# Step stores laid out per column group, two buffers for tile partials and an earlier ride load in a memory-augmented attention and SwiGLU training kernel

## The chip, the cores and the metric

The kernel runs on one core of a Trainium2 chip. The metric is the device time of one execution in microseconds (us). The engines of the core are named as in the profile: PE is the matrix engine (PEld its weight loads), DVE the vector engine, ACT the scalar engine, POOL the GpSimd engine and SP the engine that issues most transfers. Sixteen DMA engines move data between HBM and the on-chip memories.

## What is computed

The reference is a forward pass and its gradients. All tensors are bf16, with 2048 tokens of width 640, 32 heads of 128, segments of 32 tokens and 8 memory rows.

```
xn = layernorm(x)
mem = mem0                                  # 8 rows
for s in range(64):                         # segments of 32 tokens
    h = concat([mem, xn[32*s : 32*s+32]])   # 40 rows
    q, k, v = h @ Wq, h @ Wk, h @ Wv        # 32 heads
    p = softmax(mask(q @ k.T * scale))      # memory rows see all 40 rows,
    o = (p @ v) @ Wo                        # token rows those up to their own
    mem = o[:8]                             # the next segment's memory
    outs.append(o[8:])
g = silu((silu(xn @ w1) * (xn @ w3)) @ w2)
out = x + concat(outs) * g
# outputs: out and the gradients of x, mem0, Wq, Wk, Wv, Wo, w1, w3, w2 for grad_out
```

Each segment's memory comes out of the segment before, so the 64 steps are a chain, forward and, in the gradients, backward.

## The kernel before, in words

The kernel is a sequence of phases: layer norm, the gated part forward, attention forward (`phase3_Afwd`), its output (`phase3b_out`), attention backward (`phase4_Abwd`), the weight gradients of attention (`phase6_Awgrads`) and the gated part backward.

**Attention forward.** Tokens 0 to 671 get their q, k and v in an opening stage and are kept in `QVX` and `KX`. Then come 64 steps. In step `t` the function `chain` takes `hx`, 32 columns: the 8 memory rows of this segment, and 24 token rows that *ride* along, from token 672 on. `packed_half` multiplies them with half of a weight matrix so that the 128 partitions of a PSUM bank hold four groups of 32 rows: group g, row r at partition 32g + r, for columns of group g (1024 columns each). Two halves of 512 columns fill one staging tile `stg` of 128 x 1024 (lines 452 to 458), of which there are two buffers: `sk` for keys, `sq` for queries, and `sv` for values, which takes the buffer of `sk`. `dump` (line 455) stores a staging tile to DRAM on SP's queue: `sk` to `KS[t]` (467), `sq` and `sv` to the two halves of `QVS[t]` (477, 523).

From the staging tiles `packed_sel` turns the memory rows into `kT` and `qmT`; the first and second half of `sv` are copied by ACT (476, 481), and from there 8 copies on DVE fill the first rows of `vt` (484). Then follow the memory rows' scores (489), their copy `sTm` on ACT (491), two transposes (497), the maximum on DVE (499), exp, sum, `Pm` (509), transposes (514), the product with `vt` (520), the output projection `packed_out` (531), and `fold_add` and `fold_turn`, which give the next step's memory columns of `hx`. At the end `vt` gets the next segment's token rows (529).

Between these pieces stand calls `gap(...)`. They insert work on the 96 tokens of a tile of three segments (a *quad* is four heads of one tile): loads of k, q and v rows (`ld_k`, `ld`), transposes, scores, softmax, products. Those loads read the stored rows of three or four steps at once, 512 columns wide (`m_src`, `x_src`, which is `tok_src`). `in_order` at the end fixes the written order on each engine and on each queue.

**Attention backward** has the same form, from step 63 down to 0. Its opening stage (lines 766 to 790) loads the transposed weights (`WoT` first) and computes the token rows of the gradient from token 1344 on into `GX0`. Before the steps, `turn`, `dprob`, `dsoft` and `gmem_ld` run through the first 19 quads; the rest is put into the gaps. In `chain` the tile `sg` of 128 x 1024 is filled by DVE and ACT (879, 881), turned (883 to 887), and stored to `GOS[t]` (888). `loads(t - 1)` (917) brings the next step's `vT`, `Pm` and `Qst` (the queries of the memory rows, from `QVS`), `load_k(t - 1)` (933) its key rows, and `ride(t - 1)` (934) does two things: in every fourth step it loads 96 token columns into `gride` on SP's queue, and in every step POOL copies 24 of them to `gox`, the input of the next step. `gmem` (1016) computes a quad's share in the memory rows' gradients, copies it on ACT to `gks` (1025 to 1028, one buffer) and stores it to `GXP` (1029); after it, `ld_next` loads the quad four places on (`gqv`, `gor`, `gPr`, line 959). In a step, this happens in the gaps W1, G4 and G5.

Of the kernel before, what the change touches and what calls it, by code (L numbers as in the profile page):

```python
# [9 lines left out]
BF16 = mybir.dt.bfloat16  # L10
F32 = mybir.dt.float32
# [5 lines left out]
P = 128  # L17
# [23 lines left out]
class K:  # L41
# [110 lines left out]
    def setup_dram(self):  # L152
        tc = self.tc
        S, D, T, H, F = self.S, self.D, self.T, self.H, self.F
        HD = self.HD
# [14 lines left out]

        self.QVS = mk("QVS", (T, 32, 2, HD))
        self.KS = mk("KS", (T, 32, HD))
        self.GOS = mk("GOS", (T, 32, HD))
        self.NB0 = 672
# [7 lines left out]
        for tl in range(self.NTL):  # L182
# [3 lines left out]
            ns, nm = self.geo(tl)[0:2]  # L186
# [15 lines left out]
    def x_src(self, tl, w, c0, c1):  # L202
        return self.tok_src(96 * tl, self.geo(tl)[2], w, c0, c1)

    def tok_src(self, x0, nx, w, c0, c1):
        if w == "k":
            X0, XS = self.KX[:, c0:c1], self.KS[:, :, c0:c1]
        elif w == "qv":
            X0, XS = self.QVX[:, :, c0:c1], self.QVS[:, :, :, c0:c1]
        else:  # L210
            i = "qv".index(w)
            X0, XS = self.QVX[:, i, c0:c1], self.QVS[:, :, i, c0:c1]
        if x0 + nx <= self.NB0:
            return [(0, nx, X0[x0:x0 + nx])]
        out, a = [], 0
        while a < nx:
            t, r = divmod(x0 + a - self.NB0, 24)
            if r == 0 and nx - a >= 48:
                nt = (nx - a) // 24
                out.append((a, a + 24 * nt, XS[t:t + nt, 8:32]))  # L220
                a += 24 * nt
            else:
                m = min(24 - r, nx - a)
                out.append((a, a + m, XS[t, 8 + r:8 + r + m]))
                a += m
        return out

    def m_src(self, tl, w, c0, c1):
        ns = self.geo(tl)[0]
        XS = {"k": self.KS, "g": self.GOS}.get(w)  # L230
        if XS is None:
            XS = self.QVS if w == "qv" else self.QVS[:, :, "qv".index(w)]
        if w == "qv":
            return XS[3 * tl:3 * tl + ns, 0:8, :, c0:c1]
        return XS[3 * tl:3 * tl + ns, 0:8, c0:c1]

    def g_src(self, tl, c0, c1):
        nx = self.geo(tl)[2]
        x0 = 96 * tl
        if x0 >= self.GB0:  # L240
            return [(0, nx, self.GX0[x0 - self.GB0:x0 - self.GB0 + nx, c0:c1])]
        return [(0, 96, self.GOS[8 + 4 * tl:12 + 4 * tl, 8:32, c0:c1])]

# [120 lines left out]
def phase3_Afwd(k):  # L364
    nc, tc = k.nc, k.tc
    D, DC, S, H, HD, T = k.D, k.DC, k.S, k.H, k.HD, k.T
    with tc.tile_pool(name="aw", bufs=1) as wp:
# [34 lines left out]
        with tc.tile_pool(name="ast", bufs=1) as st, tc.tile_pool(name="achain", bufs=1) as ch, \  # L402
# [39 lines left out]
            def chain(t, gap):  # L442
# [12 lines left out]
                def dump(sg, dst, q=nc.sync):  # L455
                    q.dma_start(dst.rearrange("r (g c) -> g r c", g=4), sg[:])
                sk = stage()
# [18 lines left out]
                k.copy(sv[:, 0:512], bA[:], eng='s')  # L476
                dump(sq, k.QVS[t, :, 0])
                packed_half(k, bB, hx, Wv, 1)
# [43 lines left out]
                nc.vector.tensor_copy(oTm[:], pom[:])  # L522
                dump(sv, k.QVS[t, :, 1], nc.sync)
                if t + 1 == T:
# [237 lines left out]
def phase4_Abwd(k, out2):  # L762
    nc, tc = k.nc, k.tc
    D, DC, S, H, HD, T = k.D, k.DC, k.S, k.H, k.HD, k.T
    out2f = out2.flatten_outer_dims()
    with tc.tile_pool(name="gw", bufs=1) as wp:
        WoT = wp.tile([P, DC, HD], BF16, name="WoT")
        k.dma(WoT[:], k.WOT.rearrange("(dc p) j -> p dc j", p=P))
# [23 lines left out]
        with tc.tile_pool(name="gst", bufs=1) as st, tc.tile_pool(name="gchain", bufs=1) as ch, \  # L792
# [24 lines left out]

            def ride(t):
                if t < 8:
                    return  # L820
                b, sub = (t - 8) // 4, (t - 8) % 4
                if sub == 3:
                    rt = ch.tile([P, DC, 96], BF16, name="gride", tag="gride")
                    nc.sync.dma_start(rt[:], k.GST[:, 96 * b:96 * b + 96].rearrange("(dc p) s -> p dc s", p=P))
                    rides[b] = rt
                nc.gpsimd.tensor_copy(goxs[t % 2][:, :, 8:32], rides[b][:, :, 24 * sub:24 * sub + 24])

            def loads(t):
                tl, s = t // 3, t % 3
                ns, nm, nx, n = k.geo(tl)  # L830
                vT = ch.tile([P, H, 40], BF16, name="vTt", tag="vTt", bufs=1)
                nc.sync.dma_start(vT[:], k.VTD[tl][:, s])
                Pm = ch.tile([P, 2, 40], BF16, name="gPm", tag="gPm", bufs=2)
                nc.sync.dma_start(Pm[:], k.PM[t].rearrange("p (a c) -> p a c", a=2))
                Qst = ch.tile([P, 2, P], BF16, name="Qst", tag="Qst", bufs=2)
                for a in range(2):
                    nc.sync.dma_start(Qst[:, a, :], k.QVS[t, 0:8, 0, a * 2048:(a + 1) * 2048])
                ins[t] = vT, Pm, Qst

            def load_k(t):  # L840
                kr = ch.tile([40, HD], BF16, name="krow", tag="krow", bufs=1)
                nc.sync.dma_start(kr[0:8, :], k.KS[t, 0:8, :])
                k.load_x(kr, 8, k.tok_src(32 * t, 32, "k", 0, HD), nc.sync)
                krs[t] = kr

            def load_xp(t):
                xp = ch.tile([P, 8, 2, 32], F32, name="xp", tag="xp", bufs=1)
                nc.sync.dma_start(xp[:], k.GXP[t // 3, :, :, t % 3])
                xps[t] = xp
# [8 lines left out]
            def chain(t, gap):  # L858
# [27 lines left out]
                for a in range(2):  # L886
                    nc.vector.tensor_copy(gmT[:, a].rearrange("p q (g j) -> p j g q", g=2), pg[:, :, 2 * a:2 * a + 2, :])
                nc.sync.dma_start(k.GOS[t].rearrange("r (g c) -> g r c", g=4), sg[:])
                gap("W1")
# [19 lines left out]
                nc.vector.tensor_reduce(Dm[:], pr[:], axis=AX.X, op=ALU.add)  # L909
                u = ch.tile([P, 2, 40], F32, name="gu", tag="gu")  # L910
                nc.vector.tensor_tensor(u[:], ps2[:], bc_last(Dm[:], 40), ALU.subtract)
# [9 lines left out]
                for a in range(2):  # L921
                    nc.tensor.transpose(ps3[:, a, :], dS[:, a, :], k.ident[:])
                dST = ch.tile([40, 2, 8, 16], BF16, name="dSTm", tag="dSTm")
                nc.scalar.copy(dST[:].rearrange("p a q h -> p a (q h)"), ps3[:])
# [91 lines left out]
            def gmem(tl, qd):  # L1016
# [5 lines left out]
                for j in range(4):  # L1022
                    nc.tensor.matmul(pk[:, 0, j, :], qv[0:n, 0, j * P:(j + 1) * P], dS[0:n, j, 0:nm], start=True, stop=True)
                    nc.tensor.matmul(pk[:, 1, j, :], gor[0:n, j * P:(j + 1) * P], Pr[0:n, j, 0:nm], start=True, stop=True)
                ks = fl.tile([P, ns, 2, 4, 8], F32, name="gks", tag="gks", bufs=1)
                for i in range(2):
# [647 lines left out]
```

## Time and profile before

| | |
|---|---|
| median of 3 runs | 6858.57 us (6856.48 to 6860.1) |
| the profiled execution | 6865.93 us |
| its span | 6863.8 us |
| PE busy | 5507.1 us, 80% |
| PEld busy | 3209.3 us, 47% |
| DVE busy | 2423.3 us, 35% |
| ACT busy | 1884.3 us, 27% |
| POOL busy | 987.8 us, 14% |
| moved by DMA | 876.37 MB, 128 GB/s |
| mean granted PE clock | 0.883 |

How to read the rows that follow. A row of the timeline has the start and the duration in us, the engine (SPq is SP's queue of transfers), the line, the operation, what it writes and reads, how many were merged, and in brackets how long the engine had stood idle and what released it. A row of the waits has the engine and what it wanted to do, an arrow to what released it, the total in us, how often, and the longest. A row of a line or tile has the shortest, median and longest duration in ns, and the first and last start in us. In the DMA view the time asked for is cut into 40 equal slices: a digit is the share of the 16 DMA engines that were busy in that slice, in tenths, and below it stand the GB/s moved. The granted clock is 1.00 where PE ran at full speed and 0.50 where it ran at half.

### The profile page before, as it was taken

Reading aid. Unit: us, or ns where it says so; the run is one execution under the profiler, and the core shown is the slowest. Engines: PE = TensorE matmul, PEld = TensorE weight load, DVE = VectorE, ACT = ScalarE, POOL = GpSimd, SP = SyncE. Lnnn points to the kernel's source line nnn. Section 1 sums busy time; section 2 is a strip of 40 time slices with the busy share of each in tenths; the row PEclk is TensorE's granted clock in tenths of the full one; section 3 lists DMA queues with packets and bytes.
Section 4 is the critical chain, followed back from the end, with each engine's and each line's share of the span. In section 5 each row is a group of like instructions: output and inputs, shape, how many; then the busy total and the mean of one; then the engine's idle time right before and its main releaser. Section 6 shows DMA issues by size and latency. Waiting matters only on the chain. (4 is left out here: it accounts for less than half of the span.)

```text
span 6863.8 us, 167869 instructions
## 1 busy us (share of the span) xinstructions
PE 5507.1 (80%) x68068; PEld 3209.3 (47%) x68620; DVE 2423.3 (35%) x7541; ACT 1884.3 (27%) x5180; POOL 987.8 (14%) x1507
## 2 busy tenths in 40 slices
PE   6877888888886874887778884998899998775688
PEld 3444544444443543555555553555555555342244
DVE  5423544444443213444344431222222222021752
ACT  3332444433433212222222221222222222010301
POOL 0000333323233101232223320000000000000000
PEclk9888998888887886888888987999999999886799
DMA  6474444333334464665556655223322233555673
GB/s 191 149 263 120 122 120 111 103 104 104 104 106 134 124 197 113 158 157 145 142 146 164 165 129 95 78 78 95 78 79 77 77 86 87 112 155 179 194 174 94
DMA packets 1038695, 876.37 MB, mean 128 GB/s; under 512 B 525449, under 2 KB 941033, under 8 KB 1028705
## 3 DMA queue, kind: packets, MB, share of 16 engines
q1 hardware_dynamic: 656570, 568.18, 29.9%
q10 hardware_dynamic: 337894, 213.14, 11.5%
q0 software_dynamic: 43456, 84.28, 5.4%
q8 instruction: 540, 8.85, 0.6%
q14 instruction: 235, 1.92, 0.1%
HBM read 556.09 MB, written 309.09 MB: 126 GB/s over the span
## 5 line engine op out<-in xcount | busy, mean ns | idle before, releaser
L1207 PE MATMUL wg<-gr,hr 120*128 120x512 bf16 (+1 forms) x2640 | 578.4, 379 | 1.0 <-DVE ghacc L1196 0.5
L1190 PE MATMUL g<-w,gT 128*128 128x512 bf16 x1936 | 573.0, 384 | 0.7 <-ACT gT L92 0.7
L1191 PE MATMUL g<-w,gT 128*128 128x128 bf16 x2112 | 466.6, 221 | 10.7 <-issue 1.7
L1207 PEld LDWEIGHTS <-hr 120*128 120x128 bf16 (+1 forms) x2640 | 254.0, 98 | 321.4 <-issue 22.4
L1190 PEld LDWEIGHTS <-gT 128*128 128x128 bf16 x2112 | 209.0, 99 | 220.4 <-issue 13.6
L1196 DVE TENSOR_TENSOR ghacc<-ghacc,g 120x512 f32<-120x512 f32 (+1 forms) x154 | 105.9, 687 | 567.6 <-PE g L1190 567.6
L337 PEld LDWEIGHTS <-gkv 128*8 128x8 bf16 x8192 | 215.4, 100 | 162.7 <-DVE gkv L871 33.9
L92 ACT COPY gT<-t6g 128x480 bf16<-128x480 bf16 (+1 forms) x352 | 192.0, 545 | 333.8 <-PE t6g L1181 238.3
L318 PEld LDWEIGHTS <-hx 128*32 128x32 bf16 x7680 | 179.6, 96 | 175.6 <-issue 15.8
L337 PE MATMUL gbank<-WvT,gkv 128*8 128x320 bf16 x4096 | 238.6, 413 | 26.6 <-DVE gkv L871 26.6
L90 DVE CAST stg<-bank 128x512 bf16<-128x512 f32 x256 | 176.9, 691 | 222.4 <-PE bank L318 173.7
L1200 POOL CAST gxo<-ghacc 120x640 bf16<-120x640 f32 (+1 forms) x22 | 15.8, 720 | 1591.8 <-issue 1479.2
L604 ACT ACTIVATE xP<-xsp,xnm 120x120 bf16<-120x120 f32 (+1 forms) x704 | 240.2, 366 | 12.1 <-DMA PR<-xP 6.1
L484 DVE COPY vt<-stg 8x512 bf16<-8x512 bf16 x512 | 149.0, 291 | 265.9 <-ACT stg L92 259.7
L90 DVE CAST wgo<-wg 128x512 bf16<-128x512 f32 x72 | 47.5, 688 | 543.6 <-PE wg L1207 499.0
L1232 PE MATMUL oa<-gow,orr 120*128 120x512 bf16 x704 | 196.5, 382 | 36.7 <-DMA orr<-OR 36.7
L1181 PE MATMUL t6g<-ident,gr 120*128 120x120 bf16 (+1 forms) x2112 | 187.7, 219 | 43.9 <-ACT gT L92 41.7
L983 POOL DMA_DIRECT2D VTD<-gvT x176 | 127.9, 728 | 598.5 <-ACT gvT L982 581.1
L337 PE MATMUL bank<-Wo,oTm 128*8 128x320 bf16 x4032 | 209.2, 379 | 1.3
L1191 PEld LDWEIGHTS <-gT 128*128 128x128 bf16 x2112 | 208.6, 99 | 0.3
L615 POOL TENSOR_TENSOR xP<-xP,xrz 120x480 bf16<-120x480 bf16 (+1 forms) x176 | 170.2, 967 | 172.2 <-ACT xP L604 116.0
L1465 PE MATMUL w2acc<-gzB_all,hb_tok 128*128 128x128 bf16 (+3 forms) x437 | 122.8, 434 | 87.8 <-DMA hb_tok<-HB 82.7
(314 smaller groups left out, 11548.5 us busy)
## 6 DMA issues: line engine op xcount, KB each, us to landing
QVS<-stg SPq DMA_DIRECT2D x128, 256.0 KB
gqv<-QVS SPq DMA_DIRECT2D x112, 192.0 KB
vTt<-VTD SPq DMA_DIRECT2D x64, 320.0 KB
OR<-xv POOLq DMA_DIRECT2D x168, 120.0 KB, 5.5
VTD<-gvT POOLq DMA_DIRECT2D x168, 120.0 KB, 5.7
orr<-OR SPq DMA_DIRECT2D x8, 2520.0 KB
PR<-xP POOLq DMA_DIRECT2D x168, 112.5 KB, 7.6
gPr<-PR SPq DMA_DIRECT2D x168, 112.5 KB
```

The costliest lines, as they stand in the source:

```text
L90: return nc.vector.tensor_copy(out, in_)
L92: return nc.scalar.copy(out, in_)
L318: k.nc.tensor.matmul(bank[32 * g:32 * g + 32, :], x[:, dc, :], W[:, dc, c0:c0 + 512], start=(dc == 0), stop=(dc == k.DC - 1), tile_positio ...
L337: k.nc.tensor.matmul(pm[p0:p0 + nq, 0:320], x[:, h, :], W[:, h, 320 * b:320 * b + 320], start=(first and i == 0), stop=(last and i == 15), ...
L484: nc.vector.tensor_copy(vt[0:8, c0:c0 + 512], sv[32 * g:32 * g + 8, b * 512:(b + 1) * 512])
L604: nc.scalar.activation(Pb[0:n, j, 0:n], sp[0:n, j, :], ACT.Exp, bias=nmx[0:n, j:j + 1], scale=k.scale, accum_out=Z[0:n, j:j + 1])
L615: nc.gpsimd.tensor_tensor(Pb[0:n, :, 0:n], Pb[0:n, :, 0:n], bc_last(rz[0:n], n), ALU.mult)
L1181: nc.tensor.transpose(pt[:, j, :], gr[0:n, i, j * P:(j + 1) * P], k.ident[0:n, 0:n])
L1190: nc.tensor.matmul(g5[:], gT[:, i, j, :], W[:, j, 0:512], start=f, stop=l)
L1191: nc.tensor.matmul(g1[:], gT[:, i, j, :], W[:, j, 512:640], start=f, stop=l)
L1207: nc.tensor.matmul(accs[dc][:], hr[0:n, tl, dc * P:(dc + 1) * P], grs[tl][0:n, 2 - i, :], start=(tl == 0), stop=(tl == NTL - 1))
L1232: nc.tensor.matmul(ac[j][0][:], lh, gow[0:n, tl, 0:512], start=(tl == 0), stop=(tl == NTL - 1))
```

## The change

- `QVS`, `KS` and `GOS` get a dimension for the four column groups ahead of the rows. A staging tile's partition 32g + r is then row (g, r) of the tensor, and a store names one dimension of 128 rows of 1024 elements (2 KB) where it named 4 groups of 32 rows.
- All that reads these tensors goes through a new helper `step_src`. Loads of 512 columns read the same pieces as before at other addresses. Loads of whole rows (`vt`, `krow`) read four pieces of 1024 elements per row where they read one of 4096.
- The memory rows' queries are copied at the start of the backward phase from `QVS` to a new tensor `QM`, in four transfers on SP's queue, and `Qst` is loaded from there.
- `gks` gets two buffers. `gu` and `dSTm` give up buffers of their own and share those of `gpr` and `dPT`.
- `ride` is divided: `ride_ld`, the load, is issued at the gap W0 of the step before, ahead of that gap's work; the copy stays where it was.

```
-        self.QVS = mk("QVS", (T, 32, 2, HD))
-        self.KS = mk("KS", (T, 32, HD))
-        self.GOS = mk("GOS", (T, 32, HD))
+        self.QVS = mk("QVS", (T, 4, 32, 2, 1024))
+        self.KS = mk("KS", (T, 4, 32, 1024))
+        self.GOS = mk("GOS", (T, 4, 32, 1024))
+        self.QM = mk("QM", (T, 8, HD))
...
+    def step_src(self, w, t0, t1, r0, r1, c0, c1):
+        g = c0 // 1024
+        if w == "qv":
+            return self.QVS[t0:t1, g, r0:r1, :, c0 - 1024 * g:c1 - 1024 * g]
+        XS = {"k": self.KS, "g": self.GOS}.get(w)
+        if XS is None:
+            XS = self.QVS[:, :, :, "qv".index(w)]
+        if c1 - c0 > 1024:
+            assert t1 == t0 + 1 and (c0, c1) == (0, self.HD)
+            return XS[t0, :, r0:r1, :].rearrange("g r c -> r g c")
+        return XS[t0:t1, g, r0:r1, c0 - 1024 * g:c1 - 1024 * g]
...
     def m_src(self, tl, w, c0, c1):
...
+        return self.step_src(w, 3 * tl, 3 * tl + self.geo(tl)[0], 0, 8, c0, c1)
...
                 def dump(sg, dst, q=nc.sync):
-                    q.dma_start(dst.rearrange("r (g c) -> g r c", g=4), sg[:])
+                    q.dma_start(dst.rearrange("g r c -> (g r) c"), sg[:])
...
-                dump(sq, k.QVS[t, :, 0])
+                dump(sq, k.QVS[t, :, :, 0])
...
     with tc.tile_pool(name="gw", bufs=1) as wp:
+        for g in range(4):
+            nc.sync.dma_start(k.QM[:, :, g * 1024:(g + 1) * 1024], k.QVS[:, g, 0:8, 0, :])
         WoT = wp.tile([P, DC, HD], BF16, name="WoT")
...
-            def ride(t):
+            def ride_ld(t):
                 if t < 8:
                     return
                 b, sub = (t - 8) // 4, (t - 8) % 4
                 if sub == 3:
                     rt = ch.tile([P, DC, 96], BF16, name="gride", tag="gride")
                     nc.sync.dma_start(rt[:], k.GST[:, 96 * b:96 * b + 96].rearrange("(dc p) s -> p dc s", p=P))
                     rides[b] = rt
+
+            def ride(t):
+                if t < 8:
+                    return
+                b, sub = (t - 8) // 4, (t - 8) % 4
                 nc.gpsimd.tensor_copy(goxs[t % 2][:, :, 8:32], rides[b][:, :, 24 * sub:24 * sub + 24])
...
-                    nc.sync.dma_start(Qst[:, a, :], k.QVS[t, 0:8, 0, a * 2048:(a + 1) * 2048])
+                    nc.sync.dma_start(Qst[:, a, :], k.QM[t, :, a * 2048:(a + 1) * 2048])
...
-                nc.sync.dma_start(kr[0:8, :], k.KS[t, 0:8, :])
+                nc.sync.dma_start(kr[0:8, :], k.KS[t, :, 0:8, :].rearrange("g r c -> r g c"))
...
-                nc.sync.dma_start(k.GOS[t].rearrange("r (g c) -> g r c", g=4), sg[:])
+                nc.sync.dma_start(k.GOS[t].rearrange("g r c -> (g r) c"), sg[:])
...
-                u = ch.tile([P, 2, 40], F32, name="gu", tag="gu")
+                u = ch.tile([P, 2, 40], F32, name="gu", tag="gpr")
...
-                dST = ch.tile([40, 2, 8, 16], BF16, name="dSTm", tag="dSTm")
+                dST = ch.tile([40, 2, 8, 16], BF16, name="dSTm", tag="dPT")
...
-                ks = fl.tile([P, ns, 2, 4, 8], F32, name="gks", tag="gks", bufs=1)
+                ks = fl.tile([P, ns, 2, 4, 8], F32, name="gks", tag="gks", bufs=2)
...
                     if g == "W0":
+                        ride_ld(t - 1)
                         at(turn, t, 0)
...
+            ride_ld(T - 1)
             ride(T - 1)
```

More of the change, by code (lines that the diff above doesn't have):

```diff
@@ L203, in x_src @@
         return self.tok_src(96 * tl, self.geo(tl)[2], w, c0, c1)
-    def tok_src(self, x0, nx, w, c0, c1):
[L206 to L212, printed above, removed]
+    def step_src(self, w, t0, t1, r0, r1, c0, c1):
[9 more added lines that the diff above has]
+        return XS[t0:t1, g, r0:r1, c0 - 1024 * g:c1 - 1024 * g]
+    def tok_src(self, x0, nx, w, c0, c1):
         if x0 + nx <= self.NB0:
+            X0 = self.KX[:, c0:c1] if w == "k" else self.QVX[:, :, c0:c1] if w == "qv" else self.QVX[:, "qv".index(w), c0:c1]
             return [(0, nx, X0[x0:x0 + nx])]
@@ L217, in tok_src @@
             t, r = divmod(x0 + a - self.NB0, 24)
-            if r == 0 and nx - a >= 48:
+            if r == 0 and nx - a >= 48 and c1 - c0 <= 1024:
                 nt = (nx - a) // 24
-                out.append((a, a + 24 * nt, XS[t:t + nt, 8:32]))
+                out.append((a, a + 24 * nt, self.step_src(w, t, t + nt, 8, 32, c0, c1)))
                 a += 24 * nt
@@ L223, in tok_src @@
                 m = min(24 - r, nx - a)
-                out.append((a, a + m, XS[t, 8 + r:8 + r + m]))
+                out.append((a, a + m, self.step_src(w, t, t + 1, 8 + r, 8 + r + m, c0, c1)))
                 a += m
@@ L228, in m_src @@
     def m_src(self, tl, w, c0, c1):
[L229 to L235, printed above, removed]
+        return self.step_src(w, 3 * tl, 3 * tl + self.geo(tl)[0], 0, 8, c0, c1)
     def g_src(self, tl, c0, c1):
@@ L241, in g_src @@
             return [(0, nx, self.GX0[x0 - self.GB0:x0 - self.GB0 + nx, c0:c1])]
-        return [(0, 96, self.GOS[8 + 4 * tl:12 + 4 * tl, 8:32, c0:c1])]
+        return [(0, 96, self.step_src("g", 8 + 4 * tl, 12 + 4 * tl, 8, 32, c0, c1))]
     def load_x(self, dst, off, srcs, eng):
@@ L522, in chain @@
                 nc.vector.tensor_copy(oTm[:], pom[:])
-                dump(sv, k.QVS[t, :, 1], nc.sync)
+                dump(sv, k.QVS[t, :, :, 1])
                 if t + 1 == T:
```

## The prediction, on record before the change was run

> **What bounds the kernel now.** I read the page first, then the waits of PE in the two step loops, then single steps instruction by instruction, then short windows of DMA traffic.
>
> ```profile
> span 6863.8 us, 167869 instructions
> ```
> ```profile
> L456 SPq DMA_DIRECT2D KS<-stg x64: 512/542/2542, 617.5 to 2171.0; - x64
> ```
> ```profile
> L888 SPq DMA_DIRECT2D GOS<-gstg x64: 524/544/1088, 2711.8 to 4124.7; - x64
> ```
>
> The profiled execution took 6865.93 us, 2.1 us outside its span; the median of the runs is 6858.57 us, 7.4 us less. I sum against 6865.9 and take 7.4 off at the end. One store of keys is issued per forward step and one of `GOS` per backward step, so the rows of these two lines clock the loops: 63 forward steps from 617.5 to 2171.0 us, 24.66 us each, and 63 backward steps from 2711.8 to 4124.7 us, 22.43 us each. The two loops are 43% of the span, and every step needs the one before it.
>
> ```profile
> PE bank L497 <- ACT sTm L491: 165.2, 64, 5.2
> PE bank L514 <- DVE Pm L509: 30.6, 31, 2.0
> ```
> ```profile
> 1818.76 0.54 SPq L456 DMA_DIRECT2D KS<-stg  x1
> ...
> 1827.98 1.07 ACT L92 CAST stg<-bank 128x512 bf16<-128x512 f32 x2 [5.83 <-DMA KS<-stg]
> ```
>
> In the forward loop (617 to 2185 us) PE waits longest for `sTm`, 165.2 us. The second view tells why. `stg` has two buffers and the V rows take the one that the key store reads; their copy on ACT (line 476) stands until that store has landed, here 9.22 us after its issue, and `sTm` (491) is queued behind it on ACT, the copies into `vt` (484) and then the maximum (499) behind it on DVE.
>
> ```profile
> DMA  2222223223496542223222262231232222322222
> GB/s 88 88 88 105 94 94 117 105 82 100 140 281 222 199 158 94 94 105 117 105 94 94 105 211 105 94 129 59 105 117 117 82 94 105 117 105 94 94 94 105
> ```
> ```profile
> DMA  0000000000378999999630000000000000000005
> GB/s 0 0 0 0 0 0 0 0 0 0 137 273 328 410 410 355 410 437 382 246 110 0 0 0 0 0 0 0 0 0 0 0 0 0 0 0 0 0 0 191
> ```
>
> The first pair is 1822 to 1829 us, while step stores and loads drain: most of the time two or three tenths of the 16 DMA engines work, near 100 GB/s. The second pair is the 3 us from the issue, at 2585.57 us, of a `GX` store: also 128 rows of 2 KB, but one row per partition in a single dimension. Its packets run from 0.8 to 1.6 us after issue on all engines at 350 to 437 GB/s. So 256 KB occupy four engines for about 2.5 us (262 KB at 105 GB/s), or all sixteen for about 0.7 us (at 400 GB/s).
>
> **The change, term by term.**
>
> *Forward stores.* With one merged row dimension I expect the three step stores (keys, queries, values) to run as the `GX` store does. What a step is without the wait is read from the steps that waited least, one of each remainder of t by 3, cut at the key store's issue (columns: length, then busy time of PE, PEld, DVE, ACT, POOL, granted clock, DMA share, GB/s):
>
> ```profile
> 640.51:662.33 21.82, 16.93 (x299) 8.97 (x293) 8.07 (x23) 3.77 (x10) 1.67 (x3) 0.84 0.25 65
> 774.36:796.00 21.64, 19.41 (x362) 11.36 (x360) 11.85 (x36) 11.24 (x41) 8.68 (x12) 1.00 0.50 130
> 886.66:907.92 21.26, 18.80 (x354) 11.05 (x352) 11.47 (x35) 10.64 (x40) 8.36 (x11) 1.00 0.48 124
> 930.73:951.51 20.78, 18.40 (x345) 10.51 (x343) 11.05 (x32) 8.90 (x31) 7.05 (x10) 1.00 0.45 114
> 1791.98:1818.76 26.78, 22.28 (x354) 12.32 (x352) 11.47 (x35) 10.64 (x40) 8.37 (x11) 0.81 0.36 105
> ```
>
> 21.64, 21.26 and 20.78 average 21.23 us, 3.43 below the mean; over 63 steps 216 us. Even there the copy still stood for the store:
>
> ```profile
> 936.59 1.07 ACT L92 CAST stg<-bank 128x512 bf16<-128x512 f32 x2 [2.47 <-PE xpo L632]
> ```
> ```profile
> 937.21 2.51 DVE L484 COPY vt<-stg 8x512 bf16<-8x512 bf16 x8 [1.75 <-ACT stg L92]
> 939.65 0.22 DVE L499 TENSOR_REDUCE mmx<-bank 128x2 f32<-128x80 bf16 x1
> ```
> ```profile
> 934.92 1.26 PE L318 MATMUL bank<-Wv,hx 128*32 128x512 bf16 x20
> ...
> 941.25 0.29 PE L514 MATMUL bank<-ident,Pm 128*40 128x128 bf16 x2 [1.22 <-DVE Pm L509]
> ```
>
> Both copies start at 936.59, 5.87 us after the issue at 930.72, though PE finished the second V half at 936.18. With the store landed by then, the first copy and its four `vt` copies are over, the second copy ends near 936.8, its four `vt` copies (2.51/8 each) near 938.1, and after the transposes the maximum runs near 938.3 instead of 939.65. PE's 1.22 us wait for `Pm` closes; behind line 497 it has more to do in two of three steps, so I take 1.0 us per step, 63 us. What is late next is PE itself, busy 18.4 of 20.78 us.
>
> From this I take back a half clock that short waits still bring:
>
> ```profile
> 647.74 0.22 PE L497 MATMUL bank<-ident,sTm 40*128 40x40 bf16 x2 [1.97 <-ACT sTm L491]
> ...
> 650.85 0.40 PE L514 MATMUL bank<-ident,Pm 128*40 128x128 bf16 x2 [1.84 <-DVE Pm L509]
> ```
>
> These waits of under 2 us stand in the step at 640.51, whose granted clock is 0.84. I deduct 0.4 us per step, 25 us. Forward: 216 + 63 - 25 = **254 us gained**. Bounds: 279 with no half clock; 200 if a fifth of it is lost to key stores that still land late.
>
> [...]
>
> *Backward.* Waits of PE from 2726 to 4140 us, the first step left out:
>
> ```profile
> PE gvpt L979 <- DMA gqv<-QVS: 56.0, 23, 3.7
> PE gbank L326 <- ACT gstg L92: 48.8, 31, 3.9
> ...
> PE ggpt L986 <- DMA gor<-GOS: 19.4, 23, 2.1
> ...
> PE gbank L318 <- POOL gox L826: 11.3, 8, 2.3
> ```
> ```profile
> 3227.95 0.39 ACT L1027 ACTIVATE gks<-gkp 128x96 f32<-128x96 f32 x2 [7.29 <-DMA GXP<-gks]
> ```
> ```profile
> 3228.88 0.28 PE L326 MATMUL gbank<-sel,gstg 128*128 128x32 bf16 x4 [3.92 <-ACT gstg L92]
> 3231.92 0.36 PE L979 MATMUL gvpt<-ident,gqv 120*128 120x120 bf16 x2 [2.77 <-DMA gqv<-QVS]
> ```
> ```profile
> 3109.55 0.29 PE L326 MATMUL gbank<-sel,gstg 128*128 128x32 bf16 x4 [3.58 <-ACT gstg L92]
> 3109.67 0.46 PE L979 MATMUL gvpt<-ident,gqv 120*128 120x120 bf16 x3
> ```
>
> With one `gks` buffer ACT stands until the previous partial's store has landed, and the second half of `gstg` (881) is queued behind it; line 326 then waits. A second buffer removes that. But in steps like 3228.88 PE next waits for `gqv`, whose load SP issued regardless of ACT: there the time is only handed over. In steps like 3109.55 nothing waits behind. Step by step, about 22 us are of the second kind, 26 of the first. The `GOS` store shortens its stay on the four busy engines from 2.5 to 0.7 us, so loads behind it land up to 1.8 us sooner; with waits for `gqv` or `gor` in some 31 steps, a few of them shorter than that, I take 50 us. The ride load a step ahead ends the 11.3 us. It passes SP's `GOS` store and the partials' loads, and its buffer's last reader ran a step earlier, so it waits for nothing; POOL's copy stays ahead of the dS stores and the next `bdP`, and no longer holds them. Backward: 22 + 50 + 11 = **83 us gained**. Bounds: 33 if loads land no sooner (11 if the 22 us are handed over too); 135 if the `gqv` and `gor` waits (56.0 + 19.4) and the 26 us go as well.
>
> *The copy to `QM`.* Four transfers of 1 MB, DRAM to DRAM, go on SP's queue ahead of `WoT`, where the DMA engines are full:
>
> ```profile
> 2515.50:2531.50 16.00, 9.21 (x35) 3.81 (x36) 2.08 (x3) 0.60 (x2) 0.00 (x0) 0.82 1.07 362
> 2531.50:2562.00 30.50, 19.08 (x63) 7.49 (x65) 3.46 (x5) 3.90 (x7) 0.00 (x0) 0.70 1.00 341
> ```
>
> 4.19 MB at 362 GB/s is 11.6 us, nothing hides it: **11 us lost**. No such copy is in the trace; bounds 0 (it starts while phase 3b ends) and 23 (read and write counted apart).
>
> *At nothing:* `krow` and `vt` rows are now four 2 KB pieces, with the same bytes, and are loaded a step ahead; if that cover went, each would cost its own stay, under 1 us. `gu` takes the buffer of `gpr`, written and read on DVE alone, in order; `dSTm` that of `dPT`, whose transposes precede. Phase 6 reads the same 1 KB pieces. A `GOS` store has a step to land.
>
> Sum: 6865.9 - 254 - 83 + 11 = 6540; less 7.4, **6532 us**.
>
> **The rivals.**
>
> *The four engines stay full.* The step loads of `xq`, `xv`, `kr`, `gqv` and `gor` read blocks of three or four steps as before, and the 1822 us window shows such traffic at two tenths. A store over sixteen engines still ends with its share behind those loads. Against it: in the step at 930.73 few loads precede. Then only the key store's own stay is gained, 1.8 of the 3.43 us, about half the 216: 108, backward 33, copy 23: 6866 - 118 - 7 = 6741 us. It decides if the V copies still wait 2 us or more after PE. [...]
>
> *Slower: no store is spread, and the copy isn't either.* If the pieces are cut as now, forward gains nothing, all `gks` waits are handed over, the ride gives 11, and 4.19 MB at 100 GB/s hold `WoT` for 42 us: 6866 + 31 - 7 = 6890 us. It decides at phase 4's first matmul. The `GX` window speaks against it.
>
> **How the numbers follow.** Chances: the forecast 0.84, full engines 0.12, slower 0.03, 0.01 between. Range: 6445 (279, 135 and 0: 6452 less 7) to 6650 (200 forward, 33 backward, 23 lost: 6656 less 7). It leaves out the two rivals and a little of the tails, 0.2. About 0.2%, 14 us, can be told from no change; the first two cases are faster by more. Faster 0.96, same 0.01, slower 0.03.
>
> **What would show it.** Right: in the step loop's waits, ACT `stg` no longer stands for the key store; forward steps near 20.6 us, granted clock above 0.95 there; DMA digits of 9 behind each step store; no `gks` or `gride` waits; backward steps near 21.1 us with `gqv` waits left. Wrong: ACT still released by the key store, or a PE wait for `xq`, `kr` or `vt` in its place; first matmul of line 787 later than some 12 us.

## The result and the profile after

The kernel after takes 6477.24 us (median of 4 runs, 6470.46 to 6486.2), the kernel before on the same chip 6857.98 us (6856.48 to 6860.1): a ratio of 0.9445, interval 0.9429 to 0.9462. The forecast was 6532 us. The profiled execution took 6486.2 us with a span of 6484.5 us, 379.3 us less than the span before, at a mean granted clock of 0.911.

The rows of the two stores' lines that clock the loops, in the profile after (duration in ns: shortest, median, longest; first and last start):

```profile
L458 SPq DMA_DIRECT2D KS<-stg x64: 337/343/462, 619.2 to 1892.5; - x64
```
```profile
L897 SPq DMA_DIRECT2D GOS<-gstg x64: 319/352/1807, 2441.2 to 3750.5; - x64
```

Cut at these issues, the two spans divide as follows (us; for the loops the length of one step in brackets):

| | up to the first key store | forward loop | between the loops | backward loop | rest |
|---|---|---|---|---|---|
| before | 617.5 | 1553.5 (24.66) | 540.8 | 1412.9 (22.43) | 2739.1 |
| after | 619.2 | 1273.3 (20.21) | 548.7 | 1309.3 (20.78) | 2734.0 |
| difference | +1.7 | -280.2 | +7.9 | -103.6 | -5.1 |

The same loops by windows, first before and then after (columns: length, busy time of PE, PEld, DVE, ACT, POOL with their instructions, granted clock, DMA share, GB/s):

```profile
617.50:2171.00 1553.50, 1303.25 (x21621) 729.84 (x21743) 709.42 (x2089) 625.52 (x2211) 488.77 (x660) 0.87 0.40 107
2711.80:4124.70 1412.90, 1166.52 (x24055) 770.07 (x24182) 589.82 (x2766) 381.38 (x1226) 396.82 (x683) 0.88 0.57 149
```
```profile
619.20:1892.50 1273.30, 1185.65 (x21621) 691.10 (x21743) 710.81 (x2090) 639.42 (x2211) 491.27 (x660) 0.99 0.46 131
2441.20:3750.50 1309.30, 1137.10 (x24054) 755.03 (x24180) 589.03 (x2766) 380.34 (x1226) 396.48 (x683) 0.91 0.62 161
```

The forward loop has the same 21621 recorded matmuls. Of its 280 us, 118 are PE's busy time (1303.25 to 1185.65): the matmuls themselves are quicker, as the granted clock went from 0.87 to 0.99. The other 163 us are idle time that is gone. Waits of the forward loop after, first of all engines, then of PE alone (total, times, longest):

```profile
ACT stg L92 <- DMA KS<-stg: 61.9, 25, 5.6
```
```profile
PE bank L361 <- DVE fsum L351: 31.6, 76, 0.5
PE bank L516 <- DVE Pm L511: 17.2, 33, 1.2
PE bank L499 <- ACT sTm L493: 14.8, 15, 1.7
```

PE's wait for `sTm` fell from 165.2 to 14.8 us. ACT still waits for the key store, but 25 times. That a step store is now spread shows in the 3 us from 1892.4 us, when a key store is issued (busy tenths of the 16 DMA engines; GB/s):

```profile
DMA  0111000000004899999994199956362000000000
GB/s 14 58 45 45 9 0 9 0 0 0 0 0 164 355 437 410 355 355 410 410 437 137 28 273 218 219 109 273 164 273 109 0 0 0 0 0 0 0 0 0
```

All engines work for some 0.6 us at 355 to 437 GB/s, as the `GX` store of the prediction did. The completion events of the traces agree: each of the 64 key stores has 16 of them where each had 5 before, and the last one came 2.0 us after the issue at best (5.7 before; the medians are 3.9 and 7.8). The waits of PE in the backward loop after:

```profile
PE gvpt L988 <- DMA gqv<-QVS: 40.6, 16, 6.9
PE gbank L901 <- DVE gmT L896: 32.8, 41, 1.3
PE gbank L339 <- DVE gkv L880: 27.0, 63, 0.8
PE gbank L361 <- DVE fsum L351: 24.3, 67, 0.5
...
PE ggpt L995 <- DMA gor<-GOS: 7.4, 14, 0.9
...
PE gbank L328 <- ACT gstg L92: 2.0, 4, 0.5
```

The wait for `gstg`, behind which the single `gks` buffer stood, is 2.0 us, no wait for `gride` is left, and `gqv` has 40.6 us in 16 waits.

### The profile page after: what moved, and what is told of

It is laid out like the page before. It is cut to its first block, busy times and chain, and to the rows that moved or that the text cites. A ratio compares the mean times of both kernels' runs of the same rounds, so it can differ in the third digit from the quotient of the medians.

```text
span 6484.5 us, 167849 instructions
## 1 busy us (share of the span) xinstructions
PE 5360.5 (83%) x68068; PEld 3158.2 (49%) x68620; DVE 2423.8 (37%) x7541; ACT 1896.1 (29%) x5180; POOL 990.0 (15%) x1507
## 3 DMA queue, kind: packets, MB, share of 16 engines
q14 instruction: 234, 1.92, 0.1%
## 5 line engine op out<-in xcount | busy, mean ns | idle before, releaser
L1218 PEld LDWEIGHTS <-hr 120*128 120x128 bf16 (+1 forms) x2640 | 254.0, 98 | 321.1 <-issue 22.1
L92 ACT CAST wgo<-wg 128x512 bf16<-128x512 f32 x48 | 28.1, 585 | 582.8 <-PE wg L1218 533.6
L1020 DVE SCALAR_TENSOR_TENSOR gdS<-gdp,Dx,gPr 120x120 bf16<-120x120 f32 (+1 forms) x704 | 188.8, 331 | 0.0
```

The costliest lines, as they stand in the source:

```text
L92: return nc.scalar.copy(out, in_)
L1020: nc.vector.scalar_tensor_tensor(dS[0:n, j, :], dp[0:n, j, :], Dx[0:n, j:j + 1], Pr[0:n, j, :], op0=ALU.subtract, op1=ALU.mult)
L1218: nc.tensor.matmul(accs[dc][:], hr[0:n, tl, dc * P:(dc + 1) * P], grs[tl][0:n, 2 - i, :], start=(tl == 0), stop=(tl == NTL - 1))
```

## The experiments

The theory: the gain comes from the stores' spread over sixteen engines; the rest of the change adds some 30 us. Rivals: the new places in DRAM give the gain; the small edits give more, or nothing; the step loads, which have 4 or 5 completion events each as before (a key store has 16 after and had 5 before), hold the next bound. Times are medians, each compared with runs of the kernel before on the same chip. Each kernel has one profile, and loops of the same code differ from profile to profile: the forward loop of the six kernels that share it takes 1269.6 to 1283.1 us, the backward loop of e11 1285.3 and that of e12, the same code, 1296.4. Differences of about 10 us between two loops are therefore at the edge of what these profiles can tell.

**e1, the layout without the spread.** Each group gets an unused 33rd row, so the four groups of 32 rows no longer merge into one dimension of 128.

```
-        self.KS = mk("KS", (T, 4, 32, 1024))
+        self.KS = mk("KS", (T, 4, 33, 1024))
...
-                dump(sk, k.KS[t])
+                dump(sk, k.KS[t, :, 0:32])
...
```

(`QVS` and `GOS` likewise.) 

> The changed kernel with a 33rd, unused row per column group in QVS, KS and GOS, so that the rows of a store no longer merge into one dimension of 128. If the gain comes from spreading each step store over all sixteen DMA engines (my theory), the stores go back to four engines: the key store lands some 8 us after issue in the later steps, forward steps go from 20.2 back to about 24.6 us (+280 us), the backward loop loses what the faster GOS store gave (+30 to +60 us), and the time is 6790 to 6820 us. If it comes from the new places in DRAM (rows of 2 KB side by side instead of 8 or 16 KB apart), nothing changes: 6460 to 6500 us.

Measured: 6836.12 us, ratio 0.9986 (0.9977 to 0.9995). The issue takes 542 ns again (343 after), each key store has 5 completion events again and lands 8.1 us after its issue (median), and the waits of the forward loop, all engines, are near those of before. The store's issue and two waits of e1, then the first of these waits before:

```profile
L458 SPq DMA_DIRECT2D KS<-stg x64: 509/542/1607, 615.4 to 2166.7; - x64
```
```profile
ACT stg L92 <- DMA KS<-stg: 330.8, 59, 9.7
...
PE bank L499 <- ACT sTm L493: 168.4, 63, 5.4
```
```profile
ACT stg L92 <- DMA KS<-stg: 314.2, 58, 8.7
```

The forward step is 24.62 us. Every other part of the change is in, so the forward gain is the spread alone. The total lies above the expected band: the backward loop kept 27 us (1385.9), and the stretch between the loops is 9.6 us longer than before. Four groups of 32 rows gave 24.62 us a step and 5 completion events a key store, 128 rows 20.21 us and 16.

**e2, the spread without the layout.** Before, with every step store issued as four transfers of 32 partitions.

```
-                    q.dma_start(dst.rearrange("r (g c) -> g r c", g=4), sg[:])
+                    for g in range(4):
+                        q.dma_start(dst[:, g * 1024:(g + 1) * 1024], sg[32 * g:32 * g + 32, :])
```

(The `GOS` store likewise.) 

> The kernel before, its DRAM layout kept, with each step store issued as four transfers of 32 partitions. If engines are what counts, 32 rows go over sixteen engines as well, forward steps come to 20.2 to 21.2 us, slowed a little by nine more issues on SP's queue, the GOS store lands sooner too, and the time is 6530 to 6600 us (gks and the ride load are as before). If the layout or the number of transfers is what counts, the time stays at 6840 to 6880 us.

Measured: 6557.39 us, ratio 0.9583 (0.9567 to 0.9599). Steps of 20.79 and 21.34 us. ACT's wait for `KS` falls to 73.0 us (314.2 before); that each of the small transfers runs on more engines is inferred from this and from the step, not shown. Three quarters of the gain come without any new layout. What is missing goes with SP's time (four issues of 419 ns in place of one of 343) and with the waits for `gks` and `gride`, whose edits are not in; the two were not separated.

```profile
L457 SPq DMA_DIRECT2D KS<-stg x256: 302/419/2423, 619.0 to 1930.0; - x128
```

**e3, what is left of the key store's wait.** After, with the key store issued ahead of the loads of gap W0.

```
                 half(Wk_, 1, sk, 'v')
+                dump(sk, k.KS[t])
                 gap("W0")
...
-                dump(sk, k.KS[t])
```

> The changed kernel with the key store issued before the gap W0, ahead of that gap's kr loads on SP's queue. If what is left of the wait for the key store (62 us on ACT, all in every third step) comes from the kr loads, which still run on four engines ahead of it, those steps go from some 22 to 20.1 us and the time falls by 20 to 35 us, to 6440 to 6460 us. If it comes from loads issued earlier, or if the kr loads now come late in turn and make PE wait, the time stays within 8 us of 6477 us.

Measured: 6460.36 us, ratio 0.9438 (0.9424 to 0.9452), at the upper edge of the expected band. By times it cannot be told from after; by the profiles the forward loop is 1250.1 us, 23 less than after, and ACT's wait for `KS` falls from 61.9 to 14.3 us. e12 and e13, which issue the key store at the same place, have forward loops of 1244.0 and 1250.8 us, so the gain is larger than the scatter. PE's waits there:

```profile
PE bank L361 <- DVE fsum L351: 31.4, 74, 0.5
PE bank L516 <- DVE Pm L511: 11.9, 26, 1.2
PE bank L499 <- ACT sTm L493: 1.4, 3, 0.5
```

**e4, without the copy to `QM`.** After, with the four transfers left out and `Qst` reading as many rows of `QVX`, which hold other values.

```
-        for g in range(4):
-            nc.sync.dma_start(k.QM[:, :, g * 1024:(g + 1) * 1024], k.QVS[:, g, 0:8, 0, :])
...
-                    nc.sync.dma_start(Qst[:, a, :], k.QM[t, :, a * 2048:(a + 1) * 2048])
+                    nc.sync.dma_start(Qst[:, a, :], k.QVX[8 * t:8 * t + 8, 0, a * 2048:(a + 1) * 2048])
```

> The changed kernel without the copy to QM: Qst is loaded from rows of QVX in the same shape and size, so the memory rows' queries are wrong in the backward phase and all that follows from them. If the copy costs what the stretch between the two loops lost (7.9 us), the time falls by 6 to 10 us, to about 6469 us; if it is hidden where it now runs, in the drain of the forward phase, less than 3 us; by my prediction's sum 11 us.

Measured: 6470.99 us, ratio 0.9451 (0.9433 to 0.9468): no difference from after in the times. In the profile the stretch between the loops is 534.0 us, 14.7 less than after. Where the copy runs after, and PE's waits between the loops, after and then e4:

```profile
L770 SPq DMA_DIRECT2D QM<-QVS x4: 578/578/595, 1897.9 to 1967.7; - x4
```
```profile
PE gvpt L988 <- DMA gqv<-QVS: 52.9, 18, 4.4
PE qpt L574 <- DMA xq<-QVS: 32.2, 5, 14.7
...
PE g0pb L791 <- DMA WoT<-WOT: 22.1, 1, 22.1
...
PE xpo L634 <- DMA xv<-QVS: 6.5, 5, 2.4
```
```profile
PE gvpt L986 <- DMA gqv<-QVS: 45.8, 17, 3.9
...
PE g0pb L789 <- DMA WoT<-WOT: 21.3, 1, 21.3
...
PE xpo L634 <- DMA xv<-QVS: 17.8, 3, 16.1
...
PE qpt L574 <- DMA xq<-QVS: 8.4, 2, 7.3
```

The four transfers are issued behind the last key store (1892.5), the last of them 258 us before `WoT`'s load (2225.8), among the last `xq` and `xv` loads of the forward phase. Those two waits together are 38.7 us after and 26.2 in e4; the wait for `WoT` is nearly the same. One pair of profiles overstates the cost, since after has the longest stretch of its kind: in the eight profiles with the copy (e1 aside) the stretch takes 541.1 to 548.7 us, 544.2 on average, in the four without it (before, e2, e4, e7) 533.0 to 540.8, 536.0 on average. The two waits are 37.1 to 41.3 us in the eight and 26.2 to 30.5 in the four. So the copy costs about 8 us, and it costs them there; the wait for `gqv` varies in both groups (45.4 to 53.7 and 45.8 to 50.2).

**e5, e6, e8, e7: the two small edits.** After with one `gks` buffer (e5); after with the ride load at its old place (e6); after with both undone (e8); before with only the `gks` buffer and the shared tags (e7).

```
-                ks = fl.tile([P, ns, 2, 4, 8], F32, name="gks", tag="gks", bufs=2)
+                ks = fl.tile([P, ns, 2, 4, 8], F32, name="gks", tag="gks", bufs=1)
```
```
                     load_k(t - 1)
+                    ride_ld(t - 1)
                     ride(t - 1)
...
                     if g == "W0":
-                        ride_ld(t - 1)
                         at(turn, t, 0)
```

> The kernel after, with one gks buffer instead of two; all else as after (which stood at 0.9445 of before, 6470 us if before takes 6850 here). Theory of the prediction: the second buffer is worth a net 22 us of its 47 us of gks waits, the other 26 us go over to the gqv waits behind them. Then 6485 to 6500 us, with gks waits on GXP back at some 15 or more quarters and gqv waits smaller than in the profile after. Rival 1: nothing is handed over, the whole 47 us come back: 6510 to 6525. Rival 2: the faster step stores alone make the GXP store land in time, so that the buffer is worth nothing: within 8 us of after.

> The kernel after, with the gride load put back to the end of the step, just ahead of the copy that reads it (one step in four). Theory: the load's time from issue to landing stands in the way once in four steps as it did before, worth 11 us by the waits of before: 6476 to 6488 if after would take 6470. Rival: with the stores over all engines the load lands in time anyway, or the wait for it is covered by the work of the next gap: within 5 us of after, and no gox wait on gride above 1 us in the profile.

> The kernel after without its second gks buffer and with the late gride load: the layout and the stores alone. Theory: forward loop as after (20.2 us a step), backward loop between the split stores on the old layout (1345 us) and after (1309 us), so the total is 25 to 40 us above after: 6495 to 6510. If the two small edits add nothing beside the stores: within 8 us of after. If each gives its whole wait: 58 us above, 6525 to 6535.

> The kernel before, with only the second gks buffer and the two shared tags that make room for it; stores, layout and ride as before. If the gks waits are handed over to the gqv waits in the same measure as predicted, it is 22 us faster than before (0.9968), range 6820 to 6840 with before at 6850; if nothing is handed over, 47 us (0.993). If the gks waits were caused by the narrow step store that stands ahead of them, so that the gain of the buffer shows only with the new stores, it is within 10 us of before. The forward loop must stay at 24.6 us a step.

| | time, us | ratio and interval | backward loop, us |
|---|---|---|---|
| after | 6477.24 | 0.9445 (0.9429 to 0.9462) | 1309.3 |
| e5 | 6486.83 | 0.9463 (0.9444 to 0.9481) | 1317.3 |
| e6 | 6497.96 | 0.9476 (0.9455 to 0.9497) | 1317.9 |
| e8 | 6493.3 | 0.9475 (0.9456 to 0.9495) | 1331.0 |
| before | 6857.98 | 1 | 1412.9 |
| e7 | 6832.63 | 0.9971 (0.9961 to 0.998) | 1401.1 |

By times only e7 can be told from its neighbour; e5, e6 and e8 overlap with after. e6 lies 10 us above its expected band and e8 2 us below; e5 and e7 lie within theirs. The backward loops of the profiles give the order: beside the new stores both edits together are worth 21.7 us, and each alone 8 to 14, by which of them is taken out first; singly they are little more than the scatter. Without the new stores the `gks` buffer is worth 11.8. PE's waits of the backward loop, e5 and then e7:

```profile
PE gvpt L988 <- DMA gqv<-QVS: 38.5, 16, 4.2
...
PE gbank L328 <- ACT gstg L92: 18.1, 16, 4.7
```
```profile
PE gvpt L979 <- DMA gqv<-QVS: 89.2, 22, 7.2
...
PE gbank L326 <- ACT gstg L92: 2.0, 4, 0.5
```

Without the new stores (e7) the second buffer takes the `gstg` wait from 49.3 us (before, whole loop) to 2.0, and the `gqv` wait rises from 56.0 to 89.2: 33 of 47 us are handed over. Beside the new stores (e5) there is less to gain: the `gstg` wait is 18.1 us against 2.0 with the buffer. The `gqv` wait hardly moves there (38.5 and 40.6), but the loop is only 8 us shorter, so part of the 16 us still goes into other waits, and which of them is not shown.

**e10, the loads spread as well.** After, with each load of 48 or 96 step rows cut into one transfer per step of 24 rows.

```
         for (a, b, src) in srcs:
-            eng.dma_start(dst[off + a:off + b], src)
+            if b - a >= 48 and len(src.shape) > len(dst.shape):
+                for i in range((b - a) // 24):
+                    eng.dma_start(dst[off + a + 24 * i:off + a + 24 * i + 24], src[i])
+            else:
+                eng.dma_start(dst[off + a:off + b], src)
```

> The kernel after, with every load of 96 (or 48) token rows from the step tensors cut into one transfer of 24 rows for each step, so that the loads too leave the three or four engines (kr, xq, xv in the forward loop, gqv and gor in the backward loop). Theory: what waits are left in the two loops are the loads on few engines: the key store that lands 6 to 7 us after its issue in every third of the later forward steps (61.9 us of waits for KS) and gqv at 40.6 us in the backward loop; both shrink to a third or less, and the kernel gains 40 to 80 us on after (0.933 to 0.939 of before, after being 0.9445). Rival: a transfer is issued in 0.63 us now and four small ones take some 1.2, on a queue that stood issuing from 1402.8 to 1418 of a step of 20 us; the step stores then come late behind them, the forward loop slows by 1 us a step or more, and the kernel is 20 to 100 us slower than after.

Measured: 6800.07 us, ratio 0.993 (0.9904 to 0.9956): almost the whole gain is lost, far more than the rival's 20 to 100 us. Steps of 22.29 and 22.82 us; the stretches between and behind the loops, whose loads are cut as well, are 16 and 37 us longer than after. SP's queue in a forward step of e10, and PE's longest wait in its backward loop:

```profile
1502.18 5.20 SPq L250 DMA_DIRECT2D kr<-KS  x8
1507.47 0.34 SPq L462 DMA_DIRECT2D KS<-stg  x1
1507.91 0.38 SPq L462 DMA_DIRECT2D QVS<-stg  x1
```
```profile
PE gvpt L992 <- DMA gqv<-QVS: 141.5, 25, 8.6
```

Eight small `kr` loads (an issue of one takes 0.36 us by the median) occupy SP's queue for 5.20 us ahead of a key store, where after has two in 1.30 us together. Summed over the trace's SP issues, SP is busy issuing 15.2 us of a forward step and 18.6 of a backward one (10.1 and 13.3 after). Each small load lands sooner by the trace's completion events (`kr` 2.2 us after its issue against 5.3, `gqv` some 3 against 5.3), and yet PE waits longer for `gqv` (141.5 us against 40.6). That fits a load that is issued later: the order and the number of issues on SP's queue, not the engines that move, then set the time. SP isn't full, though: in e2 it issues for 14.6 us of a forward step, and that loop is only 3% longer than after's. So the sum of the issues alone doesn't explain the loss, and which issue holds up which load was not tested. Whether wider loads would help if they cost no issues was not tried either. For a small `kr` load the issue took 0.36 us of the 2.2 us to its landing, a sixth.

**e11, e12: the half clock of the backward loop.** In the step at 2680 us of the profile after, two stretches of 3.40 us, and two products of the same size:

```profile
2684.50:2687.90 3.40, 1.92 (x46) 1.57 (x47) 1.24 (x4) 1.84 (x6) 1.47 (x2) 0.99 0.65 197
2687.90:2691.30 3.40, 3.33 (x52) 1.72 (x56) 3.06 (x19) 0.00 (x0) 0.00 (x0) 0.51 0.77 248
```
```profile
2687.97 3.93 PE L339 MATMUL gbank<-WvT,gkv 128*8 128x320 bf16 x64 [0.43 <-DVE gkv L880]
...
2693.91 2.35 PE L339 MATMUL gbank<-WkT,gkv 128*8 128x320 bf16 x64
```

PE worked 1.92 of 3.40 us, with no gap over 0.9 us, and ran the next 3.4 us at 0.51. e11 is after with three more *idle matmuls* (nobody reads their result; they keep PE busy, the 126 of after's backward loop for 0.38 us each) at the end of gap W1; e12 has this and the key store of e3.

```
-            WARM = dict(G1=1, G5=2, G6=1)
+            WARM = dict(W1=3, G1=1, G5=2, G6=1)
```

> The kernel after, with three matmuls of 512 columns whose result nobody reads put in the 0.9 us gap ahead of the dP matmuls of every backward step (as the program has them in three other places). Theory of the half clock: two short gaps of 0.9 and 0.4 us within some 4 us are what sets the clock to half for the next 3.4 us in about 45 of 64 backward steps; the WvT matmuls then take 3.93 us instead of 2.35. With the first gap filled those steps fall from 20.4 to 18.8 us, and the kernel gains 50 to 75 us on after: 0.934 to 0.937 of before. Rival: only waits of some 2 us and more bring the half clock, the low windows have another cause, and filling 0.9 us changes nothing: within 8 us of after, or a little slower by the added matmuls (64 x 0.6 us at most 40 us).

> The kernel after with the key store moved ahead of the first gap and the same three idle matmuls. The two act in different loops, so the gains add: 0.9438 less 0.007 to 0.011, some 6385 to 6420 us if before takes 6850. If the idle matmuls do nothing: 0.944, as the key store alone.

Measured: e11 6478.83 us, ratio 0.9461 (0.9438 to 0.9484), no gain that the times can tell, where 50 to 75 us were expected; e12 6440.24 us, 0.9407 (0.9388 to 0.9427), 0.003 below e3 where 0.007 to 0.011 were expected. Both missed. e11's step at the same place, and its backward loop's waits:

```profile
2687.12 2.35 PE L339 MATMUL gbank<-WvT,gkv 128*8 128x320 bf16 x64 [0.43 <-DVE gkv L880]
```
```profile
PE gvpt L988 <- DMA gqv<-QVS: 53.3, 17, 6.9
...
PE gbank L901 <- DVE gmT L896: 7.2, 22, 0.7
```

The mechanism is as expected: the `gmT` wait is filled (32.8 to 7.2 us), the product runs at full speed (2.35 us against 3.93), and steps with a half clock anywhere in them fall from 54 to 24 of 63 (27 in e12). The size is not: the loop is only 24 us shorter in e11 (1285.3) and 13 in e12 (1296.4), and the wait for `gqv` is longer in both (40.6 us after, 53.3 and 47.9), so part of the gain was handed over to the loads. Even the 24 us may be flattered: the profiled execution was the fastest of e11's four and the slowest of after's four.

**e13, the `gqv` loads issued earlier.** e12, with the loads of a quad ahead of the `GXP` store that precedes them on SP's queue, and the `xp` load behind both.

```
-                gmem(tl, qd)
+                store = gmem(tl, qd)
                 ld_next()
+                store()
...
-                        if t > 0:
-                            load_xp(t - 1)
                         at(dsoft, t, 1)
                         at(gmem_ld, t, 0)
+                        if t > 0:
+                            load_xp(t - 1)
```

> The kernel with the key store moved ahead and the three idle matmuls, and two changes of order on the SP queue of the backward loop: each quarter's gqv, gor and gPr loads are issued ahead of the GXP store of the quarter that frees their buffers, and the xp load behind both. Theory: what is left in every third backward step is a gqv load that is issued only some 3 us before the first matmul that reads it (issued at 3115.28 and landed at 3122.90 in the profile after, behind an xp load of 0.56 and a GXP store of 0.59); issued 1.3 to 2 us earlier, some 13 to 16 waits of 3 to 7 us shrink by that much, and with fewer steps at the half clock the kernel gains 20 to 40 us on the one without this: 0.935 to 0.938 of before, that one being at 0.9407. Rival: the load lands when the four engines have worked through what stands ahead of it, whenever it is issued; then the waits stay at 5 us and the time within 8 us (0.940 to 0.942).

Measured: 6414.91 us, ratio 0.9375 (0.9349 to 0.9402), within the expected band: `gqv` waits 38.2 us (47.9 in e12), a loop of 1272.2 us (1296.4 in e12, 1285.3 in e11). The theory fits, but the interval still touches that of e12 (0.9388 to 0.9427), so the gain over e12 is at the edge of what the times can tell. It is the lowest ratio of these kernels. PE's longest wait in its loop:

```profile
PE gvpt L988 <- DMA gqv<-QVS: 38.2, 12, 6.0
```

## Why the prediction was right, point by point

**Forward, 254 predicted, 280 measured.** The mechanism is shown by e1, and e2 fits it: the spread of the stores, and nothing else. The step that failed is the deduction: "From this I take back a half clock that short waits still bring". The 25 us did not come: the clock stood at 0.99, and the waits beside which the prediction had found the half clock had closed (`sTm` 165.2 to 14.8 us). Without the deduction the sum is 279, within 1 us of the measured gain, but that is luck: two errors cancel there. Three steps of the profile after, for the same t as the prediction's 21.64, 21.26 and 20.78:

```profile
757.24:777.50 20.26, 19.27 (x362) 11.39 (x360) 11.83 (x37) 11.60 (x41) 8.78 (x13) 1.00 0.51 141
856.45:876.03 19.58, 18.67 (x354) 11.09 (x352) 11.43 (x36) 11.02 (x40) 8.30 (x11) 1.00 0.50 134
896.15:915.56 19.41, 18.35 (x345) 10.52 (x343) 11.08 (x33) 9.11 (x31) 8.18 (x12) 1.00 0.49 137
```

They are 1.4 to 1.7 us shorter, where 1.0 was taken for the earlier copies. Against that, in every third step from t = 25 to 58 the key store still lands 6 to 7 us after its issue by its completion events, behind `kr` loads issued just ahead of it; these 12 steps take 22.4 us on average, the other 51 take 19.7, which costs 12 x 2.7 = 32 us. So the rival of the full engines was true in one step of three for half the loop, and e3 got 23 us back by issuing the key store ahead of the loads. That the half clock can follow short gaps is shown in the backward loop of after: 0.51 behind a stretch with 1.92 us of work in 3.40 and no gap over 0.9 us.

**Backward, 83 predicted, 104 measured.** By e8 the stores alone give 82 us (1412.9 to 1331.0), where 50 was taken for loads that land sooner: the term was mis-sized, and the loads are the smaller part of it. The loop of e8, by windows, and PE's waits in it:

```profile
2445.10:3776.10 1331.00, 1145.36 (x24054) 760.49 (x24180) 589.01 (x2766) 380.50 (x1227) 396.94 (x683) 0.90 0.61 158
```
```profile
PE gvpt L989 <- DMA gqv<-QVS: 42.2, 17, 4.4
...
PE gbank L328 <- ACT gstg L92: 13.3, 17, 2.1
PE ggpt L996 <- DMA gor<-GOS: 9.7, 14, 2.0
```

21 of its 82 us are matmuls that run quicker (PE busy 1166.52 to 1145.36, clock 0.88 to 0.90), which the prediction did not count in this loop; the other 61 are waits. The waits for `gqv` and `gor`, from which it took its 50, fell by 23.5 us only (56.0 and 19.4 before). The wait for `gstg` fell by 36 (49.3 before) with the one `gks` buffer still in place: the prediction gave that wait to the second buffer alone, and the stores' spread took most of it. By completion events the latest landing of a `GXP` store fell from 8.6 to 6.9 us after its issue, which fits; what exactly shortened this wait was not tested. So the two small edits give 22 where 33 was taken: the `gks` buffer 8 to 13 for 22, the ride load 9 to 14 for 11. "Handed over" was borne out without the new stores (e7), for 33 of 47 us where the prediction read 26 of 48; beside them the buffer ended 16 us of waits and shortened the loop by 8 (e5).

**The copy to `QM`, 11 lost predicted, 8 measured** between the loops, by the means of twelve profiles. The size is near; the place was wrong. It stands not ahead of `WoT` with full engines but in the drain of the forward phase, where it delays the last `xq` loads; PE's wait for `WoT` is 22.1 us (21.2 before).

**The sum.** 280 + 104 - 8 = 376 of the 379.3 us; the head (+1.7) and the rest (-5.1) make up the difference, and there kernels with the same code differ by as much (rests of 2734.7 us in e3 and 2727.4 in e4). The forecast lay 55 us above the measured time: 26 of them in the forward loop, 21 in the backward loop and 3 in the copy. What was put at nothing cost nothing that these profiles show: of `krow`, `vt`, `gu` and `dSTm` only `dSTm` is among PE's waits in the loops after, with 1.1 us (0.9 before).

## What to carry to other kernels

Look at how many DMA engines a transfer that someone waits for keeps busy, before looking at its bytes: 256 KB over four engines or sixteen (5 or 16 completion events a key store) was the difference between 24.6 and 20.2 us a step, and one merged dimension decided it. Then count issues: four transfers in place of one gave a little less than the new layout for the step stores (e2, 20.79 us a step against 20.21), and two or four in place of one lost nearly everything for the loads (e10, 33 issues a forward step in place of 18). When a wait is removed, ask who is late next: here gains in the backward loop went in part to `gqv` (e7, e11), and issuing its load earlier seems to have won some of it back (e13). And a faster transfer may end waits that were put down to something else: the stores' spread took most of the wait that the second `gks` buffer was meant for (e8).

## What the runs showed of the hardware that was not expected

In the traces of before and after the granted clock changed on a grid of 3.413 us: all 548 changes fall within 5 ns of one such grid per trace. Cut into such stretches, from about 70 us on, where the records of the clock begin, these traces show what goes with a change. Of 2585 stretches at full clock in which matmuls ran for at least 75% of the time, 10 were followed by half clock; of 209 in which they ran for under 55%, 186 were. At half clock, all 400 stretches with under 70% were followed by half clock, and of 269 with at least 85%, 232 by full clock. (The shares are those of the recorded matmuls, of which some are missing.) The share of a stretch tells more than one long gap: 86 of the 273 stretches after which the clock fell had no gap as long as 1 us. And the issue of a key store held SP for longer when it named two dimensions of rows: 542 ns for four groups of 32 rows (before and e1), 343 ns for the same 256 KB as 128 rows in one (after; medians of 64).
